# Seven tail projections in one pass of 128 rows, their sums split anew between GpSimd and VectorE, and a warm-up tile of half the size

## The chip, the cores and the metric

The kernel runs on one core of one Trainium2 chip. The metric is the device time of one execution in microseconds (us). Time before: 923.36 us, median of 3 runs (923.26 to 923.62). Each experiment was timed on one chip in five rounds together with the kernel before, so it is compared with the kernel before of its own set, whose medians lay at 923.0 to 923.6.

Names used below: PE is the matmul engine, DVE in the traces is VectorE, POOL is GpSimd; the ACT queue and the SP queue are the two DMA queues that ScalarE and SyncE issue loads on. An x tile is 128 rows of `x`; `wg_sb` and `wu_sb` hold the gate and up weights; a dummy is a matmul on the zeroed tile `warm`, issued only to keep the PE running before there is real work.

## The reference, cut to what matters

```
xn = layernorm(x)                                   # x: 2048 x 640, bf16
q  = xn @ wq                                        # 32 heads of 192
s  = softmax(q k^T / sqrt(192)) v @ wo              # last 512 keys of each head
g  = silu((sigmoid(xn @ w_gate) * (xn @ w_up)) @ w_down)
return x + s * g
```

The kernel works in 32 units: 8 groups of 4 heads times 4 blocks of 512 rows. A unit's output projection `@ wo` is added up over the groups in `acc`, which already holds `x + g * (groups 0 to 6)` when the last group (units 28 to 31) comes. A row tile of the last group is then finished by two elementwise steps: a product (projection times `g`, read from PSUM, written to `o_sb`) and a sum (`o_sb + acc`), and by a store.

## The kernel before

The start: loads, warm-up, first layernorm. `...` marks cuts.

```python
warm = const.tile([P, 512], BF16, name="warm")
...
        nc.vector.memset(warm[:], 0.0)

        nc.vector.memset(wg_sb[:, 0, 0:2], 0.0)      # the ACT queue's wg_sb load below must wait for this one
        load_x(0, 1)                                  # SP queue
        load_x(1, 1)                                  # SP queue
        load_f(nc.scalar, wg_sb, wg_r, 0, 4, 0, 3)    # ACT queue, 384 KB, writes what the memset wrote
        load_f(nc.sync, wg_sb, wg_r, 0, 4, 3, NCD)
        load_f(nc.sync, wu_sb, wu_r, 0, 4, 0, 3)
        load_x(2, 1)
...
        dummy(18)                                     # 18 matmuls on warm: they need only the first memset
        stats_half(0, 0)
        stats_half(0, 1)
        stats_end(0)                                  # holds stats_half(1, 0) ahead of tile 0's reciprocal
        normal(0, ((0, 3 * P), (3 * P, D)))
        stats_half(1, 1)
        turn_pe(0)                                    # first transposes on the PE
        dummy(2)
```

(The comments at the line ends are mine.)

The tail: a projection in two 64-row passes with a small "seen" copy on VectorE between them, which the second pass waits for. Two projections are interleaved by `flow`, so a projection's second pass comes after the next one's first.

```python
    def project(u, q, k, out_eng=None, add=nc.vector):
        ...
        for turn in range(2):
            for cc in range(GC):
                for i in range(2):
                    r = slice(i * H2, (i + 1) * H2)
                    half = i ^ turn
                    nc.tensor.matmul(res[:, half, :], lhsT=oT[u][r, cc, q * P:(q + 1) * P],
                                     rhs=wo[r, cc, half * HD:(half + 1) * HD], ...)
            if turn == 0:
                nc.vector.tensor_copy(seen[:, DJ + 1, :], bank[k][:, :, 0])
                yield
        if g == NG - 1:
            o = fin.tile([P, D], F32, name="o_sb", bufs=2)
            gated_rows(o, t, 0, D, res, cols)          # product, VectorE, L473
            stored_rows(o, t, 0, D, add, out_eng)      # sum, engine `add`, L478; store
...
    flow([values(u + 1, h, order[h]) for h in range(4)]
         + [project(u - 1, q, order[q], nc.scalar, nc.gpsimd) for q in range(4)]
         + [project(u, q, order[q], nc.sync, nc.gpsimd if q < 2 else nc.vector) for q in range(4)])
    last_rows()     # unit 31: eight pieces of 128 x 320, matmuls of 128 rows
```

The softmax here doesn't subtract the row's maximum and nothing guards it: scores larger than these inputs give would overflow.

## Time and profile before

| | before |
|---|---|
| PE busy, share of the span | 99% |
| ACT queue's wg_sb load issued | 1.19 us |
| VectorE starts on the second x tile | 4.19 us, no wait |
| first transposes on the PE / first gate matmuls | 5.27 / 6.21 us |
| unit 31's values start on the PE | 890.56 us |
| last matmul ends / VectorE ends / span | 916.40 / 918.62 / 921.2 us |

The start in the timeline (start in us, duration in us, engine, line, operation, tiles, count, then the idle time before it and what ended it):

```profile
0.86 0.27 DVE L165 MEMSET warm<- 128x256 uint32 x1 [0.86 <-PEq L617]
1.08 0.06 DVE L167 MEMSET wg_sb<- 128x1 uint32 x1
...
1.19 0.45 ACTq L163 DMA_DIRECT2D wg_sb<-in_B_w_gate_dram  x1
1.19 4.02 PE L190 MATMUL bank<-warm 128*128 128x256 bf16 x18 [1.19 <-DVE eps_t L182]
...
4.19 0.44 DVE L198 BATCH_NORM_STATS2 st<-x_sb 128x6 f32<-128x320 bf16 x1
...
5.27 0.71 PE L230 MATMUL bank<-ident,xn 128*128 128x128 bf16 x5
...
6.21 1.28 PE L300 MATMUL bank<-xnT,wg_sb 128*128 128x128 bf16 x20
```

The DMA queues between 1.5 and 3 us (queue, packets, MB, share of 16 engines); q1 carries the SP queue's loads, q10 the ACT queue's:

```profile
q1 hardware_dynamic: 233, 0.27, 74.5%
q10 hardware_dynamic: 1, 0.00, 0.2%
```

The x tiles go first: the ACT queue's wg_sb load, issued at 1.19 us, moved a single packet before 3 us, and both x tiles had landed before VectorE wanted the second one at 4.19 us. The chain of waits at the start runs through the wu_sb transfer:

```profile
3.17 5.28 DMA wu_sb<-in_B_w_up_dram
```

The end of the chain of waits (start, duration, what):

```profile
890.56 5.51 PE bank L443 x128
896.07 0.82 PE bank L492 x12
896.89 0.67 PE bank L443 x16
897.55 12.22 PE bank L492 x180
909.78 6.64 PE bank L525 x48
916.42 0.00 issue
916.42 0.48 DVE o_sb L473
916.90 0.80 DVE gate L478 x2
917.70 0.41 DVE o_sb L473
...
918.13 0.49 DVE gate L478
```

VectorE in the tail, the lines that matter (the first is unit 30's first product), with GpSimd's last four sums between them:

```profile
905.81 0.83 DVE L473 TENSOR_TENSOR o_sb<-bank,gate 128x640 f32<-128x640 f32 x1 [0.73 <-PE bank L492]
...
912.83 3.32 POOL L478 TENSOR_TENSOR gate<-o_sb,acc 128x320 bf16<-128x320 f32 x4 [2.94 <-DVE o_sb L473]
...
914.54 0.89 DVE L473 TENSOR_TENSOR o_sb<-bank,gate 128x320 f32<-128x320 f32 x2 [0.60 <-POOL gate L478]
915.35 1.15 DVE L478 TENSOR_TENSOR gate<-o_sb,acc 128x320 bf16<-128x320 f32 x1
```

After the last matmul VectorE still has 2.2 us of work, because it is late: it waited 0.60 us for GpSimd to free an `o_sb` buffer, and a sum that takes 0.4 to 0.5 us elsewhere took 1.15 us while GpSimd was busy with its own sums.

### The profile page before, as it was taken

Reading aid. Unit: us, or ns where it says so; the run is one execution under the profiler, and the core shown is the slowest. Engines: PE = TensorE matmul, PEld = TensorE weight load, DVE = VectorE, ACT = ScalarE, POOL = GpSimd, SP = SyncE. Lnnn points to the kernel's source line nnn. Section 1 sums busy time; section 2 is a strip of 40 time slices with the busy share of each in tenths; the row PEclk is TensorE's granted clock in tenths of the full one; section 3 lists DMA queues with packets and bytes.
Section 4 is the critical chain, followed back from the end, with each engine's and each line's share of the span. In section 5 each row is a group of like instructions: output and inputs, shape, how many; then the busy total and the mean of one; then the engine's idle time right before and its main releaser. Section 6 shows DMA issues by size and latency. Waiting matters only on the chain.

```text
span 921.2 us, 25377 instructions
## 1 busy us (share of the span) xinstructions
PE 915.1 (99%) x11540; PEld 630.2 (68%) x11540; DVE 489.8 (53%) x985; ACT 302.3 (33%) x333; POOL 138.2 (15%) x162
## 2 busy tenths in 40 slices
PE   9999999999999999999999999999999999999997
PEld 7445455466868686867676777777777767676886
DVE  5452522544646464646555555545554646464666
ACT  4222222255142424242333333232424151515150
POOL 1000100001002000200020012001100110165735
PEclk9999999999999999999999999999999999999999
DMA  9310330115444434442425162516251615273535
GB/s 319 81 30 1 89 86 1 43 62 87 78 64 108 84 62 78 93 99 42 98 85 106 36 104 79 113 29 112 73 110 37 113 61 97 60 118 106 101 76 130
DMA packets 163148, 77.15 MB, mean 84 GB/s; under 512 B 140992, under 2 KB 158608, under 8 KB 163040
## 3 DMA queue, kind: packets, MB, share of 16 engines
q1 hardware_dynamic: 155680, 53.64, 30.4%
q0 software_dynamic: 5808, 20.52, 7.6%
q8 instruction: 90, 1.47, 0.7%
q10 hardware_dynamic: 1552, 1.38, 0.5%
q14 instruction: 18, 0.15, 0.1%
HBM read 39.45 MB, written 2.62 MB: 46 GB/s over the span
## 4 chain that ended last, share of the span: by engine, by line
PE 99%; DMA 1%; SPq 0%; DVE 0%; issue 0%
PE bank L492 22%; PE bank L421 21%; PE bank L443 19%; PE bank L403 18%; PE bank L250 10%; PE bank L262 6%; PE bank L369 1%; PE bank L300 1%; PE bank L525 1%; DMA wu_sb<-in_B_w_up_dram 1%; SPq L158 0%; DVE gate L478 0%; SPq L163 0%; DVE o_sb L473 0%; PE bank L230 0%
## 5 line engine op out<-in xcount | busy, mean ns | idle before, releaser
L407 ACT ACTIVATE E<-bank 128x1024 bf16<-128x1024 f32 x256 | 255.3, 1022 | 456.5 <-PE bank L403 456.4
L421 PE MATMUL bank<-xnT,wq_sb 64*128 64x512 bf16 x1800 | 226.4, 376 | 0.0
L492 PE MATMUL bank<-wo_sb,oT 64*128 64x320 bf16 x2688 | 205.2, 296 | 0.0
L403 PE MATMUL bank<-qT,kT 64*128 64x512 bf16 x1536 | 200.8, 376 | 0.0
L443 PE MATMUL bank<-vbuf,E 64*128 64x193 bf16 x4096 | 195.4, 243 | 0.0
L443 PEld LDWEIGHTS <-E 64*128 64x128 bf16 x4096 | 178.9, 94 | 10.1 <-issue 0.3
L492 PEld LDWEIGHTS <-oT 64*128 64x128 bf16 x2976 | 164.8, 94 | 29.1
L428 DVE CAST qT<-bank 128x1024 bf16<-128x1024 f32 x90 | 110.2, 1225 | 128.5 <-PE bank L421 128.5
L421 PEld LDWEIGHTS <-wq_sb 64*128 64x128 bf16 x1800 | 106.0, 100 | 87.0 <-issue 0.4
L403 PEld LDWEIGHTS <-kT 64*128 64x128 bf16 x1536 | 88.2, 94 | 73.4
L456 DVE TENSOR_TENSOR o_st<-bank,rden 128x768 bf16<-128x768 f32 x128 | 122.6, 958 | 4.8 <-DMA out_dram<-gate 0.4
L506 DVE TENSOR_TENSOR acc<-bank,acc 128x640 f32<-128x640 f32 x96 | 79.1, 823 | 20.1 <-PE bank L492 20.1
L118 POOL DMA_DIRECT2D vbuf<-in_A_v_cache_dram x28 | 21.1, 753 | 312.6 <-PE bank L443 309.7
L426 DVE COPY seen<-bank 128x2 f32<-128x2 f32 x90 | 14.4, 160 | 79.1 <-PE bank L421 79.1
L455 DVE RECIPROCAL rden<-bank 128x4 f32<-128x4 f32 x128 | 23.4, 183 | 60.4 <-PE bank L443 59.5
L250 PE MATMUL bank<-xnT,wu_sb 128*128 128x512 bf16 x220 | 54.7, 379 | 0.0
L250 PE MATMUL bank<-xnT,wg_sb 128*128 128x512 bf16 x220 | 54.7, 379 | 0.0
L262 PE MATMUL bank<-wd_sb,hT 128*128 128x512 bf16 (+1 forms) x384 | 52.8, 299 | 0.0
L256 DVE TENSOR_TENSOR hT<-bank,sig 128x512 bf16<-128x512 f32 x44 | 30.3, 689 | 42.0 <-ACT sig L253 42.0
L253 ACT ACTIVATE sig<-bank 128x512 bf16<-128x512 f32 x44 | 26.3, 597 | 68.4 <-PE bank L250 63.7
L262 PEld LDWEIGHTS <-hT 128*128 128x128 bf16 x384 | 29.7, 98 | 23.1
L250 PEld LDWEIGHTS <-wu_sb 128*128 128x128 bf16 x220 | 21.5, 98 | 26.0
(56 smaller groups left out, 368.6 us busy)
## 6 DMA issues: line engine op xcount, KB each, us to landing
wo_sb<-in_A_wo_dram SPq DMA_DIRECT2D x7, 960.0 KB, 5.6
wq_sb<-in_A_wq_dram POOLq DMA_DIRECT2D x7, 960.0 KB, 6.1
k_st<-in_A_k_cache_dram POOLq DMA_DIRECT2D x14, 384.0 KB, 5.0
vbuf<-in_A_v_cache_dram POOLq DMA_DIRECT2D x28, 192.0 KB, 3.4
row<-in_A_x_dram POOLq DMA_DIRECT2D x16, 160.0 KB, 3.3
oT<-o_st SPq DMA_TRANSPOSE x128, 3.3
x_sb<-in_A_x_dram SPq DMA_DIRECT2D x3, 640.0 KB, 10.7
wd_sb<-in_B_w_down_dram SPq DMA_DIRECT2D x1, 1920.0 KB, 14.2
```

The costliest lines, as they stand in the source:

```text
L250: nc.tensor.matmul(bank[k][:, half, 0:r1 - r0], lhsT=w[:, c, f * P:(f + 1) * P], rhs=xnT[:, b, c, r0:r1], start=(c == 0), stop=(c == NCD - 1))
L253: nc.scalar.activation(sig[:, 0:r1 - r0], bank[k][:, 0, 0:r1 - r0], AF.Sigmoid)
L256: nc.vector.tensor_tensor(hT[b][:, f, r0:r1], bank[k][:, 1, 0:r1 - r0], sig[:, 0:r1 - r0], ALU.mult)
L262: nc.tensor.matmul(wide(k)[:, d0:d1], lhsT=hT[b][:, f, q * P:(q + 1) * P], rhs=wd_sb[:, f, d0:d1], start=(f == 0), stop=(f == NF - 1))
L403: nc.tensor.matmul(bank[k][:, i, :], lhsT=kT[r, pr, j, c * P:(c + 1) * P], rhs=q[r, pr * DJ + j, :], start=(j == 0), stop=(j == DJ - 1))
L407: nc.scalar.activation(E[u, pr][:, c, :, :], bank[k][:], AF.Exp, scale=scale_qk)
L421: nc.tensor.matmul(bank[k][:, half, :], lhsT=wq[r, c, col:col + DJ * (P - 1) + 1:DJ], rhs=xnT[r, b, c, :], start=(c == 0 and not second), ...
L428: nc.vector.tensor_copy(qT[u][:, 2 * m:2 * m + 2, :], bank[k][:])
L443: nc.tensor.matmul(o4[:, q, 0:DH + 1], lhsT=e[r, c, h % 2, q * P:(q + 1) * P], rhs=vbuf[r, h, c, 0:DH + 1], start=(turn == 0 and qq == 0 a ...
L456: nc.vector.tensor_tensor(o_st[u][:, :, h * DH:(h + 1) * DH], o4[:, :, 0:DH], rden[:].to_broadcast([P, TQ, DH]), ALU.mult)
L492: nc.tensor.matmul(res[:, half, :], lhsT=oT[u][r, cc, q * P:(q + 1) * P], rhs=wo[r, cc, half * HD:(half + 1) * HD], start=(turn == 0 and c ...
L506: nc.vector.tensor_tensor(cols(acc[:, t, :]), res, cols(acc[:, t, :]), ALU.add)
```

## The change

Its intent: seven of the eight projections of units 29 and 30 no longer need the "seen" handshake between two passes; GpSimd, slow (1.54 us for a 128x640 sum where VectorE takes 0.82) and in VectorE's way, gets only the four sums of unit 29 and one half sum of unit 31; and the warm-up tile, of which the dummies read only 256 columns, is made that size.

```diff
-    warm = const.tile([P, 512], BF16, name="warm")
+    warm = const.tile([P, 256], BF16, name="warm")
@@ project
-        for turn in range(2):
+        for turn in range(2 if two else 1):
-                    r = slice(i * H2, (i + 1) * H2)
+                    r = slice(i * H2, (i + 1) * H2) if two else slice(0, P)
-            if turn == 0:
+            if two and turn == 0:
@@ last_rows
-                args = (o, t, d0, d1, nc.gpsimd if q < 2 else nc.vector, (nc.scalar, nc.sync)[i])
-                if q < 2:
-                    stored_rows(*args)
-                    continue
+                args = (o, t, d0, d1, nc.vector if q or i else nc.gpsimd, (nc.scalar, nc.sync)[i])
                 wait.append(args)
-                while len(wait) > (1 if (q, i) < (3, 0) else 0):
+                while len(wait) > (1 if (q, i) > (0, 0) and (q, i) < (TQ - 1, 1) else 0):
@@ the tail
-         + [project(u - 1, q, order[q], nc.scalar, nc.gpsimd) for q in range(4)]
-         + [project(u, q, order[q], nc.sync, nc.gpsimd if q < 2 else nc.vector) for q in range(4)])
+         + [project(u - 1, 0, order[0], nc.scalar, nc.gpsimd)])
+    for q in range(1, 4):
+        next(project(u - 1, q, order[q], nc.scalar, nc.gpsimd, False))
+    for q in range(4):
+        next(project(u, q, order[q], nc.sync, nc.vector, False))
```

(Start and stop flags of the matmuls, cut here, follow.)

More of the change, by code (lines that the diff above doesn't have):

```diff
@@ L479, in stored_rows, with project @@
         out_eng.dma_start(of[t * P:(t + 1) * P, d0:d1], r_sb)
-    def project(u, q, k, out_eng=None, add=nc.vector):
+    def project(u, q, k, out_eng=None, add=nc.vector, two=True):
         g, b = u // NB, u % NB
@@ L494, in project @@
                                      start=(turn == 0 and cc == 0),
-                                     stop=(turn == 1 and cc == GC - 1), skip_group_check=True)
-            if turn == 0:
+                                     stop=(cc == GC - 1 and (turn == 1 or not two)),
+                                     skip_group_check=two)
+            if two and turn == 0:
                 nc.vector.tensor_copy(seen[:, DJ + 1, :], bank[k][:, :, 0])
```

## The prediction

> **What bounds it now.** PE is 99% busy on the page, and 99% of the chain that ended last. The chain of waits in order of time shows, at the end: the 64-row projections of units 29/30 to 909.78 us, the 128-row last rows (48 matmuls, 6.64 us) to 916.42, then VectorE alone to 918.62 (product, two sums, product, sum: 2.2 us), then stores to 921.2. The VectorE timeline shows why: at 914.5 it waited 0.60 us for GpSimd to free an o_sb buffer, and the sum at 915.35 took 1.15 us where its unblocked likes take about 0.4 to 0.49, ending just after GpSimd's sums (912.83 to about 916.15). VectorE is about 1.2 us late when the PE ends. [...]
>
> **Removed, added, moved.**
> 1. Seven of eight tail projections go from 24 64-row matmuls to 12 of 128 rows. From the chain: 64-row, 12.22 us/180 = 67.9 ns, 1.63 us a projection; 128-row, 6.64/48 = 138 ns, 1.66 us. So +0.03 us each, about +0.2 us in all, on the critical path. [...] the chain shows no visible gap at 909.78.
> 2. Seven hidden "seen" copies (0.16 us each on VectorE) vanish.
> 3. GpSimd keeps unit 29's four sums (1.54 us each, at a pace of 1.66, fits) and one half sum. VectorE gains two sums of 0.82 and three of about 0.43 us. For unit 30 VectorE needs product 0.86 + sum 0.75 = 1.6 us per 1.66 us of PE: it just keeps up. In the last rows it needs about 0.41 + 0.41 per 0.83 us of PE: also just.
> 4. After the last matmul: one product and two sums, 0.40 + 0.40 + 0.49 = about 1.3 us in place of 2.2.
> 5. Unit 31's transposes wait for unit 29's projections, so start about 0.7 us earlier (903.4 against 904.1). No gain: nobody waited for them.
> 6. Half the warm-up memset (0.27 us) saves about 0.13 us before the dummies. The chain at the start runs through the SP queue's loads and the wu_sb transfer (landing at 8.45), not through it: 0 to 0.05 us.
>
> **Sum.** PE end 916.42 + 0.2 = 916.6; VectorE end about 917.95 in place of 918.62; stores behind unchanged (2.6 us). Saving about 0.65 us, 0.07%. Predicted 922.7 us, 8 in 10 within 922.1 to 923.5. Chances: faster by over 2% 0.01, within 2% 0.98, slower by over 2% 0.01.
>
> **What would show it.** Tail projections at about 138 ns per 128x320 matmul with no PE idle; PE end near 916.6; VectorE end near 918.0 with no wait on GpSimd after 907; no VectorE sum of 320 columns above 0.6 us; unit 31's transposes from about 903.4; same start up to 8.5 us.
>
> **What would make it wrong.** VectorE has almost no slack from 905 to 917: if a GpSimd sum overlaps the first unit 30 sum (906) or the half sum blocks one at 913, the delay carries to the end and eats the gain. The first projection's second pass now follows its first by one values pass only, so a late "seen" copy would stall the PE by up to 0.2 us. If 128-row matmuls that alternate between two banks run slower than the last rows' 138 ns, the loss is 84 matmuls times the difference.

## More of the kernel before

The two-element memset of `wg_sb` is there only to be waited for: it holds the ACT queue's load back. On VectorE that small memset stands behind the warm-up memset, and the load goes out 0.11 us after the small memset starts (1.08 and 1.19 us in the kernel before, 0.95 and 1.06 us in the changed one), so the load's time of issue depends on the length of the memset in front.

## The result, and the profile after

The changed kernel took 923.15 us, median of six runs (922.88 to 925.02); the kernel before 923.38 us (923.02 to 923.70), also six. The ratio is 1.0003, with a 95% interval of 0.9990 to 1.0016: the same. (Ratios are the mean time of one kernel's runs over the mean of the other's of the same rounds, so not quite the ratio of the medians.) The median lies inside the predicted range, but the drop of 0.65 us that was predicted is not there, and there is something new: the six runs are 922.88, 923.06, 923.15, 923.15, 924.61 and 925.02. The kernel before had no run above 923.70. Below, where a kernel's runs fall into two groups over 1 us apart, they are called the lower kind (here 922.88 to 923.15) and the upper kind (here 924.61 and 925.02).

The profiled run, 922.88 us, is of the lower kind. The start, in the timeline:

```profile
0.84 0.17 DVE L165 MEMSET warm<- 128x128 uint32 x1 [0.84 <-PEq L618]
0.95 0.06 DVE L167 MEMSET wg_sb<- 128x1 uint32 x1
...
1.06 0.45 ACTq L163 DMA_DIRECT2D wg_sb<-in_B_w_gate_dram  x1
1.06 4.02 PE L190 MATMUL bank<-warm 128*128 128x256 bf16 x18 [1.06 <-DVE eps_t L182]
...
4.99 0.49 DVE L198 BATCH_NORM_STATS2 st<-x_sb 128x6 f32<-128x320 bf16 x1 [0.79 <-DMA x_sb<-in_A_x_dram]
...
6.01 0.54 PE L230 MATMUL bank<-ident,xn 128*128 128x128 bf16 x5 [0.93 <-DVE xn L218]
...
6.92 1.28 PE L300 MATMUL bank<-xnT,wg_sb 128*128 128x128 bf16 x20
```

The DMA queues between 1.5 and 3 us:

```profile
q1 hardware_dynamic: 145, 0.17, 42.5%
q10 hardware_dynamic: 48, 0.05, 21.4%
```

The shorter memset let the ACT queue's wg_sb load out at 1.06 us in place of 1.19: it had been level with the SP queue's load of the second x tile (issued at 1.20 us in both) and is now 0.14 us ahead of it. By 3 us it has moved 48 packets where it had moved 1, and the SP queue's loads 145 where they had moved 233. The chain of waits at the start has changed its path from the wu_sb transfer to the second x tile:

```profile
1.20 3.76 DMA x_sb<-in_A_x_dram
```

VectorE waits 0.79 us for this tile; since its statistics stand in VectorE's order ahead of the first tile's reciprocal, the first tile is late too, the PE idles 0.93 us, and the first gate matmuls start at 6.92 us, 0.71 us later than before.

The end of the chain of waits:

```profile
891.27 5.51 PE bank L443 x128
896.78 0.82 PE bank L492 x12
897.60 0.67 PE bank L443 x16
898.26 12.36 PE bank L492 x96
910.62 4.09 PE bank L526 x30
914.71 0.04 DVEq L473
...
917.28 0.40 DVE o_sb L473
917.68 0.40 DVE gate L478
918.08 0.40 DVEq L629
```

Unit 31's values start at 891.27 us, again 0.71 us late: nothing between 7 and 890 us gave it back. VectorE in the tail:

```profile
905.84 0.83 DVE L473 TENSOR_TENSOR o_sb<-bank,gate 128x640 f32<-128x640 f32 x1 [0.80 <-PE bank L492]
906.70 0.82 DVE L478 TENSOR_TENSOR gate<-o_sb,acc 128x640 bf16<-128x640 f32 x1
...
913.51 0.52 DVE L478 TENSOR_TENSOR gate<-o_sb,acc 128x320 bf16<-128x320 f32 x1
...
917.20 0.48 DVE L473 TENSOR_TENSOR o_sb<-bank,gate 128x320 f32<-128x320 f32 x1
917.60 0.88 DVE L478 TENSOR_TENSOR gate<-o_sb,acc 128x320 bf16<-128x320 f32 x2
```

The wait for GpSimd and the long sum are gone, and after the last matmul (910.46 + 6.68 = 917.14 us, by the timeline) VectorE has one product and two sums left, 1.3 us. Counted from the start of unit 31's values, VectorE ends after 918.48 - 891.27 = 27.21 us, where the kernel before took 918.62 - 890.56 = 28.06 us. So the tail is 0.85 us shorter, the head is 0.71 us longer, and in a third of the runs something costs 1.5 to 2 us more.

### The profile page after: what moved, and what is told of

The parts are those of the page before. It is cut to its first block, busy times and chain, and to the rows that moved or that the text cites. A ratio compares the mean times of both kernels' runs of the same rounds, so it can differ in the third digit from the quotient of the medians. Undisturbed runs are those within 1.5% of the kernel's fastest.

```text
span 921.1 us, 25176 instructions
## 1 busy us (share of the span) xinstructions
PE 913.9 (99%) x11438; PEld 630.7 (68%) x11456; DVE 490.7 (53%) x983; ACT 302.7 (33%) x333; POOL 132.7 (14%) x157
## 4 chain that ended last, share of the span: by engine, by line
PE 98%; DVE 1%; DMA 0%; issue 0%; ACT 0%; DVEq 0%; SPq 0%
PE bank L492 22%; PE bank L421 21%; PE bank L443 19%; PE bank L403 18%; PE bank L250 10%; PE bank L262 6%; PE bank L369 1%; PE bank L300 1%; PE bank L526 0%; DMA x_sb<-in_A_x_dram 0%; DVE gate L478 0%; DVE o_sb L473 0%; DVE st L198 0%; PE bank L230 0%; DVE xn L218 0%
## 5 line engine op out<-in xcount | busy, mean ns | idle before, releaser
L492 PEld LDWEIGHTS <-oT 64*128 64x128 bf16 (+1 forms) x2892 | 164.3, 94 | 29.8 <-issue 0.3
L262 PE MATMUL bank<-wd_sb,hT 128*128 128x128 bf16 (+1 forms) x376 | 52.4, 297 | 0.4
```

Of the source, the lines that this page charges most:

```text
L262: nc.tensor.matmul(wide(k)[:, d0:d1], lhsT=hT[b][:, f, q * P:(q + 1) * P], rhs=wd_sb[:, f, d0:d1], start=(f == 0), stop=(f == NF - 1))
```

## The experiments

Theory A: the tail gains about 0.8 us, and the shorter memset, by letting the ACT queue's load out early, takes it away at the start. Rival B: the start differs by chance from run to run. Rival C: the dummies on the PE end earlier, and the PE is slower afterwards (the two upper runs had a mean granted clock of 0.998 and 0.997, the other four 0.999 or 1.000); that the one follows from the other was a guess of mine, which no trace had shown. Twelve experiments were run (b3 is the changed kernel again); all gave correct results. What the traces of their profiled runs show of the start, in us:

| kernel | wg_sb issued (ACT queue) | VectorE starts on x tile 1 (wait) | dummies end | first transposes | first gate matmuls | five runs, us |
|---|---|---|---|---|---|---|
| before | 1.19 | 4.19 (none) | 5.21 | 5.27 | 6.21 | 922.9 to 923.9, but for two (see d1) |
| after | 1.06 | 4.99 (0.79) | 5.08 | 6.01 | 6.92 | see above |
| a1_tail_only | 1.19 | 4.49 (0.16) | 5.21 | 5.52 | 6.47 | 922.18 to 922.78 |
| a2_warm_only | 1.06 | 5.04 (0.88) | 5.08 | 6.07 | 6.98 | 923.75, 924.10, 925.00, 925.09, 925.47 |
| a3_gate_late | 1.19 | 4.21 (none) | 4.97 | 5.28 | 6.19 | 922.10 to 922.49, and 924.17 |
| a4_gate_early | 0.90 | 5.19 (0.96) | 4.99 | 6.22 | 7.13 | 923.85, 923.90, 924.19, 925.13, 925.39 |
| b1_x1_on_act | 1.18 | 4.94 (x tile 0 is late) | 5.08 | 6.02 | 6.97 | 922.85, and 924.02 to 924.44 |
| b2_more_dummies | 1.06 | 5.11 (0.91) | 5.91 | 6.14 | 7.05 | 923.16 to 923.88 |
| b3_after_again | 1.06 | 5.62 (1.37) | 5.08 | 6.65 | 7.60 | 923.32, 923.44, 924.38, 924.63, 924.88 |

(In a3 and a4 the dummies end early for their start because the PE reached its fast rate during the last of them: 18 took 3.91 and 3.76 us, in the kernel before 4.02; see "Why two kinds of runs".)

### a1_tail_only: the change without the smaller tile

```diff
-    warm = const.tile([P, 256], BF16, name="warm")
+    warm = const.tile([P, 512], BF16, name="warm")
```

> The changed kernel with the warm-up tile at its old size of 512, so only the tail is changed. Theory A (the tail gained about 0.8 us as the two profiles show from the common point at the start of unit 31's values to the end, and the smaller warm-up memset lets the ACT queue's wg_sb load go out 0.13 us before the second x tile's load, which then lands late): x_sb of tile 1 lands by about 4.2 us as before, about 922.5 us, ratio to before 0.9990 to 0.9993, small spread. Rival B (start differs by chance from run to run): same median and spread as the changed kernel, some runs near 925. Rival C (dummies on the PE end earlier [...]): as A here, told apart by a3 and a4.

Measured: 922.37 us median, before 923.16 us (nine runs, 923.01 to 923.54), ratio 0.9991 with an interval of 0.9979 to 1.0004. The interval touches 1, but the five runs (922.18 to 922.78) lie below all nine of before. The tail is again 27.21 us long (918.03 - 890.82). The second x tile was 0.16 us late even here, so there is some chance in its landing, but far less than the change brought. Theory A holds, B in its strong form does not.

### a2_warm_only: the kernel before with only the smaller tile

```diff
-    warm = const.tile([P, 512], BF16, name="warm")
+    warm = const.tile([P, 256], BF16, name="warm")
```

> The kernel before with the warm-up tile of 256 only. Theory A and rival C: slower than before by 0.6 to 2 us (about 924 to 925), first transposes at about 6.0 us in place of 5.26, x_sb tile 1 landing near 5 us. Rival B: same as before, 923.4.

Measured: 925.00 us median, ratio 1.0019 (1.0005 to 1.0032), all five runs above all nine of before. The first transposes came at 6.07 us, the second x tile at 5.04, as expected. One line of the change, which saves 0.1 us of VectorE work, costs 0.6 to 0.9 us in the better runs and about 2 us in the others. B has fallen.

### a3_gate_late: the change, dummies early, load late

```diff
         nc.vector.memset(warm[:], 0.0)
+        nc.vector.memset(pause[:], 0.0)              # pause: another [P, 256] tile
         nc.vector.memset(wg_sb[:, 0, 0:2], 0.0)
```

> The changed kernel with its 256-wide warm-up tile, so the dummies start early, but with another 256-wide memset ahead of the two-element one that the ACT queue's wg_sb load waits for, so that load is issued at about 1.19 us as before. Theory A: x_sb tile 1 lands by about 4.2 us, 922.5 us as a1. Rival C: as the changed kernel, 923.1 or more, with some runs at a lower clock. Rival B: as the changed kernel.

Measured: 922.38 us median, four runs at 922.10 to 922.49 and one at 924.17. The dummies start at 1.06 us as in the changed kernel, the load goes out at 1.19 us as in the kernel before, and the delay of the second x tile is gone (VectorE starts on it at 4.21 us). So it is the time of the load that delays the tile, not the time of the dummies. But the one run at 924.17, whose mean granted clock was 1.000, kept C alive for the second kind of runs.

### a4_gate_early: the kernel before, load early

```diff
+        nc.vector.memset(wg_sb[:, 0, 0:2], 0.0)
         nc.vector.memset(warm[:], 0.0)
-        nc.vector.memset(wg_sb[:, 0, 0:2], 0.0)
```

> The kernel before, warm-up tile of 512, but the two-element memset that the ACT queue's wg_sb load waits for put ahead of the warm-up memset: the load goes out at about 0.95 us, the dummies start as before or 0.03 us later. Theory A: slower than before by 0.6 us or more (924 to 925.5), x_sb tile 1 landing at 5 us or later. Rivals B and C: same as before, 923.4.

Measured: 924.19 us median, ratio 1.0014 (1.0001 to 1.0027), all five runs above all of before. Nothing of the warm-up was changed but the order of two memsets. That settles the head: the load's issue relative to the x tiles sets when the second x tile lands (VectorE starts on it at 5.19 us with the load out at 0.90, at 4.19 us with the load out at 1.19). Both a2 and a4 again show two kinds of runs, about 1.3 us apart (923.75 to 924.19 and 925.00 to 925.47).

### b1_x1_on_act: the second x tile's load ahead of wg_sb, on the ACT queue

```diff
-        load_x(1, 1)
+        load_x(1, 1, nc.scalar)                      # the ACT queue's first instruction
```

> The changed kernel with one more edit: the second x tile's load is issued by the ACT queue at the very start, ahead of that queue's wg_sb load, which then no longer competes with it. Theory A (the early wg_sb packets delay x tile 1): x tile 1 lands by about 3.6 us, VectorE does not wait for it, the start is as in a3 or up to 0.3 us earlier, 921.9 to 922.4 us, in all runs. If the runs above 924 of the changed kernel come from the same delay of x tile 1, they are gone; if they come from the PE's clock alone, one or two of five stay near 924.

Measured: 924.12 us median, one run at 922.85, four at 924.02 to 924.44, with a mean granted clock of 0.999 or 1.000 in all five: a miss. With both x tiles issued at 0.74 us, and wg_sb's two loads behind them from 1.18 us, the first tile landed late: VectorE started on it at 3.89 us, where the kernel before and the changed one start at 3.14 and 3.06, and that tile heads the chain. Moving the competitor from the second tile to the first is no cure. It brought the same idle PE (0.94 us), and the profiled run, 924.12 us, shows what the second kind of run is: its first 20 gate matmuls took 2.33 us in place of 1.28.

### b3_after_again: the changed kernel again

> The changed kernel again, on the chip of b1 and b2, for the two modes: about 923.1 in most runs and 924.6 to 925 in one to three of five; x tile 1 landing at 4.9 to 5.1 us in the profile.

Measured: 924.38 us median, ratio 1.0011 (0.9999 to 1.0024); two runs near 923.4, three at 924.38 to 924.88. This time the profiled run was of the upper kind. Its start in the timeline:

```profile
1.06 4.02 PE L190 MATMUL bank<-warm 128*128 128x256 bf16 x18 [1.06 <-DVE eps_t L182]
...
5.62 0.49 DVE L198 BATCH_NORM_STATS2 st<-x_sb 128x6 f32<-128x320 bf16 x1 [1.37 <-DMA x_sb<-in_A_x_dram]
...
6.65 0.71 PE L230 MATMUL bank<-ident,xn 128*128 128x128 bf16 x5 [1.57 <-DVE xn L218]
...
7.60 2.33 PE L300 MATMUL bank<-xnT,wg_sb 128*128 128x128 bf16 x20
```

The second x tile was later than in the first profile (5.62 against 4.99 us), the PE idle for 1.57 us, and the same 20 matmuls took 2.33 us in place of 1.28: about half rate.

### b2_more_dummies: the change with a longer warm-up

```diff
-        dummy(18)
+        dummy(25)
```

> The changed kernel with 25 in place of 18 warm-up matmuls, which fill the PE's idle time up to about 5.8 us while x tile 1 is still late. If the runs above 924 come from the PE idling [...] (theory C for the second mode): median 923.1, none above 923.6. If they come from the data (x tile 1 or wg_sb later still): as the changed kernel, one to three of five near 924.6 to 925.

Measured, on the chip of b3: 923.55 us median, 923.16 to 923.88, no run above 924. The second x tile was as late as ever, but the PE was not idle:

```profile
1.06 4.85 PE L190 MATMUL bank<-warm 128*128 128x256 bf16 x25 [1.06 <-DVE eps_t L182]
...
5.11 0.50 DVE L198 BATCH_NORM_STATS2 st<-x_sb 128x6 f32<-128x320 bf16 x1 [0.91 <-DMA x_sb<-in_A_x_dram]
...
6.14 0.54 PE L230 MATMUL bank<-ident,xn 128*128 128x128 bf16 x5 [0.23 <-DVE xn L218]
...
7.05 1.28 PE L300 MATMUL bank<-xnT,wg_sb 128*128 128x128 bf16 x20 [0.15 <-DVE xnT L234]
```

So with that time filled by dummies none of five runs was of the upper kind, against three of five for b3 in the same set, while the late data remain and keep their 0.7 us or more. That ties the upper kind to the idle PE between the dummies and the first transposes, though five runs each are few. The median came out 0.4 us above what was expected and one run above the 923.6 set as the limit; the profiled run shows part of that elsewhere, a sum of unit 28 on VectorE of 2.06 us at 881 us (see the last section).

### d1_fewer_dummies: the kernel before with a shorter warm-up

```diff
-        dummy(18)
+        dummy(14)
```

> The kernel before with 14 in place of 18 warm-up matmuls and nothing else: the loads are as before (x tile 1 landing by about 4.2 us), but the PE idles from about 4.2 us to the first transposes at 5.3, about 1 us. Theory (the mode above 924 is the PE at about half rate after it idled for 0.9 us or more, whatever made it idle): in several of the five runs the first 20 gate matmuls take about 2.3 us in place of 1.28 and the time is 924.2 to 924.8. Rival (that mode comes from late data): all runs as before, 923.0 to 923.6.

Measured: 923.52, 923.69, 924.45, 924.58 and 925.41 us. The x tiles were in time (4.34 us), the PE idle for 1.16 us before the transposes, and three of five runs are of the upper kind, as expected. But two of the nine runs of the kernel before were too (924.36 and 925.02), as none had been in any set so far, not even on this same chip in the set of b1 to b3; and the profiled run, 923.52 us, had its 20 matmuls at 1.28 us in spite of the idle time. The 0.9 us in this theory and in c1's was my estimate from the idle times of b1 and b3 (0.94 and 1.57 us); no such limit is shown, for 0.93, 0.99, 1.16 and 1.23 us in the profiles of the changed kernel, a2, d1 and a4 were followed by transposes at the fast rate (0.54 us for five). The result agrees with an idle PE as a cause but does not prove it, and the two slow runs of the kernel before suggest that it is not the only one.

### b4_sums_only: the tail, first half

```diff
-         + [project(u, q, order[q], nc.sync, nc.gpsimd if q < 2 else nc.vector) for q in range(4)])
+         + [project(u, q, order[q], nc.sync, nc.vector) for q in range(4)])
```

with the change's `last_rows`, in the kernel before.

> The kernel before with only the sums moved as in the change (unit 30's on VectorE, one half sum of the last rows on GpSimd, the rest deferred by one on VectorE); projections stay in two 64-row passes, warm-up tile 512. Theory (the tail's gain is VectorE no longer waiting for GpSimd): nearly all of the gain of a1, 922.3 to 922.6 us, ratio 0.9990 to 0.9993; one product and two sums (1.3 us) after the last matmul. Rival (the gain comes from the one-pass projections): as before, 923.2.

Measured: 923.42 us median (922.89 to 923.58), before 923.04 us, ratio 1.0001 (0.9987 to 1.0014): nothing gained. My account of the tail's gain fell here. The list of the PE's waits from 886 us has one line:

```profile
PE bank L492 <- DVE seen L497: 0.3, 1, 0.3
```

With unit 30's sums on VectorE, the "seen" copies that a projection's second pass waits for stand behind them in VectorE's order, and the PE waits for VectorE. Counted from start to start of its matmuls, that one wait cost 0.49 us (0.61 us where the step is otherwise 0.12), which is how much later b4's PE ends in the table below (26.33 against 25.84). So b4 removes VectorE's wait for GpSimd and puts another wait in its place.

### b5_pass_only: the tail, other half

```diff
-    for q in range(4):
-        next(project(u, q, order[q], nc.sync, nc.vector, False))
+    for q in range(4):
+        next(project(u, q, order[q], nc.sync, nc.gpsimd if q < 2 else nc.vector, False))
```

in the changed kernel, with the old `last_rows` and the old warm-up tile.

> The kernel before with only the seven tail projections in one pass of 128 rows; sums stay on GpSimd and VectorE as before, warm-up tile 512. Theory: no gain, PE end later by 0.1 to 0.2 us, VectorE again about 1.2 us late at the PE's end, 923.2 to 923.5 us. Rival: the gain of a1, 922.4.

Measured: 922.53 us median (922.29 to 922.85), before 923.04 us (nine runs from 923.01), ratio 0.9992 (0.9979 to 1.0005), ranges apart. The rival was right: most of the tail's gain comes with the one-pass projections, which I had booked as a loss on the PE. The traces show how. All times from the start of unit 31's values:

| kernel | unit 30's first product starts | last matmul ends | VectorE ends |
|---|---|---|---|
| before | 15.25 | 25.84 | 28.06 |
| b4_sums_only | 15.25 | 26.33 | 27.95 |
| b5_pass_only | 14.57 | 25.87 | 27.43 |
| after (a1 the same) | 14.57 | 25.87 | 27.21 |

The PE needs the same time in both forms. But two interleaved projections finish late: the second pass of each comes after the first pass of the next, so its rows are complete 0.68 us later than when the projections follow one another whole. VectorE and GpSimd, which are the late ones in the tail, get these projections 0.54 us (the first) to about 0.7 us earlier. b5 also takes the seven "seen" copies off VectorE, and no run separates the two; but in the kernel before each copy stood in time in which VectorE then still waited 0.73 us for the PE, so the copies' 0.16 us each are hardly the gain. The end of b5's chain shows VectorE less late than before: at its last product it is 0.6 us behind the last matmul (917.32 against 916.76), where the kernel before is 1.2 us behind (917.62 against 916.40). Moving the sums then gives the remaining 0.22 us. (The parts depend on the order: sums first gives 0.11 us, and one pass then 0.74.)

### c1_gate_later_dummies and c2_tail_dummies: towards a better version

c1 is the changed kernel with a later load and two more dummies:

```diff
+        nc.vector.memset(pause[:], 0.0)              # pause: another [P, 512] tile
         nc.vector.memset(wg_sb[:, 0, 0:2], 0.0)
-        dummy(18)
+        dummy(20)
```

> The changed kernel with its 256-wide warm-up tile, a 512-wide memset ahead of the two-element one (the ACT queue's wg_sb load at about 1.3 us, 0.1 us later than in a3) and 20 in place of 18 warm-up matmuls. Theory (wg_sb's packets must come behind both x tiles, and the PE must not idle for about 0.9 us or more before the first transposes): x tile 1 never waited for by VectorE beyond 4.3 us, no run in the mode above 924, median 922.0 to 922.4, ratio 0.9988 to 0.9992 with the smallest spread of all. If wg_sb now comes too late, the first gate matmuls wait for it at 6.2 us and the gain is lost.

c2 is a1 with `dummy(20)`.

> a1 (the change without the smaller warm-up tile) with 20 in place of 18 warm-up matmuls. Theory: as a1, 922.2 to 922.5, no run above 923; says whether c1's later gate is worth anything beyond the old 512-wide tile.

Measured: c1 922.38 us median (922.29 to 922.81), c2 922.49 us (922.34 to 923.01), before 923.33 us (nine runs, 923.03 to 923.82); ratios 0.9991 both, with intervals of 0.9978 to 1.0003 and 0.9978 to 1.0005. No run of the upper kind in ten. c1's profiled run shows the limit on the other side: issued at 1.32 us, wg_sb was waited for by the first gate matmuls (0.30 us at 6.46). c2's profiled run, its slowest at 923.01, waited 0.48 us for wu_sb at 8.19 us with the load at its old time, so landings also vary by chance. In these profiles, between 1.06 us, too early, and 1.32 us, somewhat too late, the old 1.19 us was about right, and a later gate is worth nothing more. All versions with the changed tail and a load not issued early (a1, a3, c1, c2) have medians of 922.4 to 922.5 us, about 0.1% below both kernels; each interval still reaches 1. a1, the change without its first line, is the simplest of them.

## Why the prediction was right or wrong

**The step that failed is 6**: "Half the warm-up memset (0.27 us) saves about 0.13 us before the dummies. The chain at the start runs through the SP queue's loads and the wu_sb transfer (landing at 8.45), not through it: 0 to 0.05 us." In its place the runs show a loss of 0.71 us in the better runs (first gate matmuls at 6.92 against 6.21 us), and about 1.3 us on top of that in some (b3: its three upper runs average 924.63, its two lower 923.38). In the kernel before, the chain did run through the wu_sb transfer; after the change it ran through the second x tile (3.76 us, landing at 4.96). So the wrong part of the step is the path: it was taken to stay where it was. What I did not ask is what the memset, being in front, held back: the two-element memset behind it gates a 384 KB load, and the chain was free of the x tiles only because that load's packets came after theirs. a2 and a4 show the loss with nothing else changed, a3 shows it gone with the gate alone put back.

**Why two kinds of runs**: in the profiles of the upper kind (b1, b3) the PE works at about half rate after idling (2.33 us for 20 matmuls against 1.28, after 0.94 and 1.57 us). It had not lost a fast rate by idling; it had not reached it yet. The 18 dummies took 4.02 us in the kernel before, the changed one and b3 alike, 0.22 us each, while the seven more in b2 took only 0.83 us (4.85 - 4.02), 0.12 us each. By the starts of single matmuls, the PE is at its fast rate within 2.7 to 5.0 us of the first dummy in twelve of the fourteen profiles, and only after 8.5 us in b1 and 9.3 us in b3; until then all their matmuls are slow. In the changed kernel's first profile the rise fell into the idle 0.93 us, so the transposes behind it already ran fast (0.54 us for five, against 0.71 in the kernel before and in b3). That idling between dummies and transposes can put the rise off is supported by b2 and not proven. It is not needed for a slow run either: a3 had one (924.17) and the kernel before two, with 0.3 us idle or less in the profiled runs of both; those slow runs have no profile, and their cause stays open.

What sets the moment of the rise is not shown. The traces show about half the rate at the start of every profile (0.22 us a dummy against 0.12 in the last seven of b2), a rise whose time differs between runs, and that an idle time of 0.93 us was followed by fast matmuls in one profile (the changed kernel's first) and 0.94 us by slow ones in another (b1). The views' granted clock does not show the change of rate: it reads 1.00 while the dummies run slow and in b3's slow stretch, and the mean clock of the upper runs (0.997 and 0.998 in the first set, 0.999 or 1.000 in the others) is hardly below that of the lower ones (0.999 to 1.000).

**Step 1**, PE end 0.2 us later: 0.03 us later (25.87 against 25.84). By their starts, 128-row matmuls follow one another every 136 ns, and so do pairs of 64-row ones, so the one-pass form costs the PE nothing. The estimate of 138 ns came from dividing 6.64 us by 48, and that stretch holds the change from 64 to 128 rows: the first 128-row matmul starts 229 ns after the last 64-row one, where the next pair would have started after 117. The chain does not show this 0.11 us, because it counts a matmul as busy until its modelled end. Both kernels pay it once in the tail, at different places.

**Steps 3 and 4**, VectorE ends about 0.65 us earlier: right in sum, even modest (0.85 us), with 1.3 us left after the last matmul as predicted. That is partly luck, for the reason given was only partly right. I put the gain on VectorE no longer waiting for GpSimd; b4 did that without the one-pass form and gained 0.11 us in the trace and nothing in time. Of the 0.85 us, 0.63 came with the one-pass form alone (b5), by completing the projections 0.5 to 0.7 us earlier. The other 0.22 us came with the sums on VectorE, which cost the PE nothing here because no "seen" copy stands behind them any more. Step 2 called these copies "hidden"; they were, but only as long as VectorE had no sums to do between them.

**VectorE and GpSimd sums at the same time**: in the kernel before, the VectorE sum that ran beside GpSimd's sums took 1.15 us; like sums after the change took 0.48 us. What holds such a sum up is not shown. But in the order of b5 and then the sums, removing the overlap was the smaller part of the gain (0.22 of 0.85 us).

**Step 5**, transposes of unit 31 0.7 us earlier, without gain: counted from the start of unit 31's values they start at 12.86 us in place of 13.54 (904.13 and 904.10 us in the traces), and nobody waited for them in either.

## What to carry to other kernels

Before shortening or moving an instruction that "costs nothing", list what waits behind it: here 0.13 us of memset was the only thing that kept a large load behind two small urgent ones. An engine that is off the critical path for work can be on it for order. And when a stage's end is set by the engine that empties the PE's results, count when each result is complete, not only how long the PE takes for all of them: two interleaved passes cost the PE nothing and handed the projections over 0.5 to 0.7 us later.

## What the traces show of the hardware

- Loads of two queues side by side: between 1.5 and 3 us, 48 of the ACT queue's packets among 145 of the SP queue's in the changed kernel, against 1 and 233 before. An issue 0.13 us earlier of a 384 KB load made VectorE wait 0.8 us for a 160 KB one that it had not waited for.
- The PE's rate at the start: the matmuls at half rate (2.33 against 1.28 us for 20) after idle times of 0.94 and 1.57 us (b1, b3) came before the PE's first rise, as the slow dummies show. The rise came within 2.7 to 5.0 us of the first dummy in twelve profiles, and only after 8.5 and 9.3 us in b1 and b3. Two of the twelve were already fast when they idled (1.16 us in d1, 1.23 us in a4) and still fast after it; in two more the rise fell into the idle time (0.93 us in the changed kernel, 0.99 us in a2).
- A sum on VectorE beside one on GpSimd: a 128x640 sum on VectorE, 0.82 us alone, took 2.06 us in the profiled run of b2, where GpSimd had started a sum 0.01 us before it (1.40 us; waiting that out first would make about 2.2, an estimate from 1.40 + 0.82), and the PE waited for what came after it:

```profile
881.11 1.40 POOL L512 TENSOR_TENSOR acc<-acc,row 128x640 f32<-128x640 f32 x1 [0.79 <-DMA row<-in_A_x_dram]
881.12 2.06 DVE L478 TENSOR_TENSOR gate<-o_sb,acc 128x640 bf16<-128x640 f32 x1
...
883.97 0.84 PE L443 MATMUL bank<-vbuf,E 64*128 64x193 bf16 x16 [0.39 <-DVE o_sb L473]
```

- A change of rows in the PE: at the change from 64 to 128 rows the next matmul starts 229 ns after the last one in both traces, 0.11 us more than the 117 ns to the next pair of 64-row matmuls; the chain of waits does not show it. Apart from that a projection of 24 64-row matmuls takes as long as one of 12 of 128 rows (12 steps of 136 ns each, 1.63 us).
